# Full-array matmuls ahead of the scores in slots with few jobs: attention and a bilinear GLU on one core

## The chip, the core and the metric

The kernel runs on one core of a Trainium2 chip. The metric is the time of one execution on the device in microseconds, the median of several runs. Beside it stands one profiled execution with the records of every engine: TensorE (PE, with its weight loads as PEld), VectorE (DVE), ScalarE (ACT), GpSimd (POOL) and SyncE (SP), which issues the DMAs.

## The reference

One layer on x of 2048 rows and 640 columns, in bfloat16: attention with 32 heads of 20 columns behind a layer norm, then a bilinear GLU of inner width 1728 behind another.

```python
qkv = layernorm(x) @ wqkv                       # 3 x 32 heads x 20
p = softmax(q @ k.T * 20 ** -0.5)               # per head, 2048 x 2048
h = x + (p @ v) @ wo
g, u = layernorm(h) @ w_gate, layernorm(h) @ w_up
out = h + (g * u) @ w_down
```

## The kernel before, in words

Heads lie in eight groups of four, each head in a strip of 32 rows (20 used). For a group, a block of 512 queries and a tile of 128 keys, a score matmul takes one strip of kT as weights and one strip of the queries as moving data (L427); it uses a quarter of the array's rows, and the strips of different heads can run beside each other. Three such results of 512 columns (or six of 256 in the last passes) fill a **score tile** `sc` of 128 x 1536 in PSUM. There are two such tiles, so the scores of tile i wait until the exponential of tile i-2 has read its own. ScalarE turns each of the 656 score tiles into a tile E of exponentials (L433). A matmul per head and key tile then multiplies E by the values (L597, 32 output columns, a quarter of the array too) and sums in the bank `acc`, four in a batch.

The main loop takes one score tile per **slot**. In each slot it issues, in this order, the scores and the exponential (`emit_S`), goes on with an open job up to a budget of 640 nominal ns (`go_on`), issues a batch of value matmuls of an earlier tile (`emit_AV`), runs events that are due (the norms' DMAs) and pieces of VectorE work, and, where the job was at its end, begins another up to 440 nominal ns (`begin`) or one of the "x" pieces, which make some of the exponentials on VectorE from scores in the bank `mi` (L453 to L477). TensorE works in program order, so this is its order.

**Jobs** are all the other matmuls: projections of q and k (L270), of v (L284), transposes (L252), the output projection (L812), the GLU's two products (L878) and its last one (L911). They are generators that yield nominal costs: 216 for a matmul of 512 columns, 136 for one of 320, 300 for a job of five transposes, 680 for a job of v. Marks such as NEXT and END carry no cost. All jobs share one PSUM bank, `mi`, so the next one waits until VectorE has emptied it. `step` fetches the next cost from the current job. Jobs come in queues: projections first, then, when all norms of a block of queries are there, its tail (output projection, layer norm, GLU). Between a tail's end and the next block's norms there are few or none, as before the first transposes of a tail. The norms of the last groups of a pass run as urgent jobs with float32 matmuls (L539, L551).

`ident` is the 128 x 128 identity in bfloat16, `kT[0]` holds the keys of group 0 and is complete after the first chunks. `keep_busy(WARM)` (L640 to L643) issues 58 matmuls of the identity by itself into one place of a score tile before the loop, in the time in which the first input arrives. WARM, 58, also serves the change as the index of a tile. Behind the loop comes the last tail, with PSUM banks of its own.

## Time and profile before

| | |
|---|---|
| median of 3 runs | 977.72 us (975.7 to 977.83) |
| profiled execution, its span | 977.6 us |
| TensorE busy | 865.3 us (89%), 6981 matmuls recorded |
| ScalarE busy | 905.2 us (93%), of it exponentials 887.8 |
| VectorE busy | 576.8 us (59%) |
| scores L427 | 2352 matmuls, 1456 of them 32x512 |
| values L597 | 2432 matmuls |
| granted TensorE clock, mean over the span | 0.935 |

Busy times are unions of the records of an engine; the mean of one instruction can be longer than its distance from the next, as they overlap: one exponential lasts 1.66 us on record, and 656 of them fill 887.8 us. The row PEclk has the clock that the throttle granted to TensorE in 40 equal slices of 24.4 us, in tenths of full speed. In a list of waits, "A <- B" is idle time of A that ended when B was done.

### The profile page before, as it was taken

The page shows a single profiled execution, that of the slowest core. Times are in us where ns is not written, and L with a number is a line of the kernel's source. Part 1 is how long each engine was busy: PE and PEld are TensorE (multiplying, and loading weights), DVE is VectorE, ACT ScalarE, POOL GpSimd, SP SyncE. Part 2 cuts the span into 40 slices and gives each one's busy share as a digit, 9 for nine tenths or more (in the row PEclk, how much of TensorE's full clock was granted, in tenths as well). Part 3 has the DMA queues.
Part 4 walks back from the last instruction along what each step waited for, and adds up shares of the span by engine and source line. Part 5 has one row for each costly group of instructions (what it writes and reads, how often), then busy time and mean ns, then how long its engine had stood idle before and what let it go on. Part 6 is the DMA issues. An engine that isn't in the chain of part 4 may idle for free.

```text
span 977.6 us, 17623 instructions
## 1 busy us (share of the span) xinstructions
PE 865.3 (89%) x6981; PEld 325.1 (33%) x7041; DVE 576.8 (59%) x1186; ACT 905.2 (93%) x692; POOL 64.6 (7%) x163
## 2 busy tenths in 40 slices
PE   6779998889989899999898988898889999989987
PEld 4223332222223222233232222233332333435455
DVE  7564367877777777777677677777143331143232
ACT  6689999999999899999999999999899999999941
POOL 4110001200000000000000000000000000000000
PEclk9999999999999599999778899999597999989989
DMA  6000000010014022101420222000602000211210
GB/s 182 4 24 1 1 25 24 13 32 27 5 47 146 12 66 59 40 13 33 180 67 12 66 67 60 12 22 23 163 1 66 14 13 20 67 36 40 81 35 17
DMA packets 67816, 44.42 MB, mean 45 GB/s; under 512 B 18504, under 2 KB 63404, under 8 KB 67728
## 3 DMA queue, kind: packets, MB, share of 16 engines
q1 hardware_dynamic: 67728, 43.23, 15.5%
q8 instruction: 57, 0.93, 0.4%
q14 instruction: 31, 0.25, 0.1%
HBM read 35.91 MB, written 7.30 MB: 44 GB/s over the span
## 4 chain that ended last, share of the span: by engine, by line
ACT 44%; PE 32%; issue 13%; DVE 9%; POOL 1%; ACTq 0%; DVEq 0%; POOLq 0%
ACT E L433 44%; PE sc L427 8%; PE acc L597 6%; PE mi L878 3%; PE mi L270 3%; PE mi L812 2%; PE mi L284 2%; PE mi L911 2%; PE f L878 2%; DVE xv L463 1%; PE mi L453 1%; DVE st L176 1%; PE f L911 1%; PE mi L252 1%; DVE vx L239 1%
## 5 line engine op out<-in xcount | busy, mean ns | idle before, releaser
L433 ACT ACTIVATE E<-sc 128x1536 bf16<-128x1536 f32 x656 | 887.8, 1662 | 30.4 <-PE sc L427 29.7
L427 PE MATMUL sc<-qa,kT 32*128 32x512 bf16 x1456 | 205.9, 406 | 41.3 <-ACT E L433 35.0
L597 PE MATMUL acc<-E,vx 128*32 128x512 bf16 (+1 forms) x2352 | 215.6, 374 | 5.3 <-DVE vx L239 4.1
L427 PEld LDWEIGHTS <-kT 32*128 32x128 bf16 x2352 | 89.8, 92 | 260.8 <-issue 251.0
L597 PEld LDWEIGHTS <-vx 128*32 128x32 bf16 x2432 | 56.6, 94 | 159.7 <-issue 151.9
L270 PE MATMUL mi<-lnT,wp 128*128 128x512 bf16 x282 | 84.7, 382 | 9.7 <-DVE kT L277 2.3
L427 PE MATMUL sc<-qb,kT 32*128 32x256 bf16 (+1 forms) x896 | 72.0, 301 | 13.8 <-ACT E L433 13.0
L529 POOL TENSOR_TENSOR on<-asb,bc 128x512 bf16<-128x512 f32 (+1 forms) x30 | 34.5, 1150 | 714.7 <-DMA bc<-scr 507.1
L463 DVE TENSOR_SCALAR xv<-mi 128x512 int32<-128x512 f32 x80 | 55.0, 688 | 29.9 <-PE mi L453 26.3
L911 PE MATMUL mi<-wd,hh 128*128 128x320 bf16 x378 | 68.4, 303 | 3.6 <-DVE xv L463 3.5
L239 DVE CAST u<-mi 128x512 bf16<-128x512 f32 (+3 forms) x56 | 34.9, 624 | 56.2 <-PE mi L878 56.0
L886 DVE TENSOR_TENSOR hh<-mi,u 128x512 bf16<-128x512 f32 (+3 forms) x56 | 34.9, 624 | 55.0 <-PE mi L878 54.9
L878 PE MATMUL mi<-ln2T,wu 128*128 128x512 bf16 (+2 forms) x188 | 55.2, 385 | 4.6 <-DVE xv L463 3.0
L468 DVE SCALAR_TENSOR_TENSOR xe<-xt,xv 128x512 bf16<-128x512 f32 x80 | 56.6, 707 | 2.0
L477 DVE SCALAR_TENSOR_TENSOR xt<-xt,xm 128x512 f32<-128x512 f32 x80 | 56.3, 704 | 0.9
L476 DVE SCALAR_TENSOR_TENSOR xt<-xm 128x512 f32<-128x512 f32 x80 | 55.7, 697 | 0.0
L878 PE MATMUL mi<-ln2T,wg 128*128 128x512 bf16 (+2 forms) x187 | 52.3, 372 | 2.2 <-issue 0.8
L911 PEld LDWEIGHTS <-hh 128*128 128x128 bf16 x448 | 37.5, 97 | 40.1 <-issue 29.8
L915 DVE TENSOR_TENSOR xr<-mi,xr 128x320 bf16<-128x320 f32 x27 | 13.3, 492 | 51.3 <-PE mi L911 51.3
L812 PE MATMUL mi<-wo,on 128*128 128x320 bf16 x224 | 41.8, 311 | 0.7 <-DVE xv L463 0.4
L607 DVE COPY asb<-acc 128x512 f32<-128x512 f32 (+1 forms) x34 | 20.2, 594 | 34.5 <-PE acc L597 32.3
L277 DVE TENSOR_SCALAR kT<-mi,one_row 128x512 bf16<-128x512 f32 x31 | 23.2, 749 | 29.0 <-PE mi L270 29.0
(143 smaller groups left out, 637.0 us busy)
## 6 DMA issues: line engine op xcount, KB each, us to landing
bc<-scr SPq DMA_DIRECT2D x100, 64.0 KB
wu<-in_B_w_up_dram SPq DMA_DIRECT2D x20, 320.0 KB
wg<-in_B_w_gate_dram SPq DMA_DIRECT2D x20, 320.0 KB
qsp<-qa SPq DMA_DIRECT2D x8, 384.0 KB
xr<-in_A_x_dram SPq DMA_DIRECT2D x16, 160.0 KB
out_dram<-xr SPq DMA_DIRECT2D x14, 160.0 KB
wd<-in_B_w_down_dram SPq DMA_DIRECT2D x13, 160.0 KB
xs<-in_A_x_dram SPq DMA_DIRECT2D x3, 640.0 KB
```

The costliest lines, as they stand in the source:

```text
L239: nc.vector.tensor_copy(dst, src)
L270: nc.tensor.matmul(ps[:], lhsT=wslice(m, g, c), rhs=lnT[:, c, ch * QB:(ch + 1) * QB], start=(c == 0), stop=(c == KT - 1))
L427: nc.tensor.matmul(sc[:, o:o + w], lhsT=kT[g][SLOT * j:SLOT * (j + 1), kt * P:(kt + 1) * P], rhs=q_of(g, b, c0, w)[SLOT * j:SLOT * (j + 1) ...
L433: nc.scalar.activation(e[:, 0:n], sc[:, 0:n], ACT.Exp, bias=EXP_BIAS, scale=SM_SCALE)
L463: nc.vector.tensor_scalar(v[:], ps[:], X_SCALE, 0.0, ALU.mult, ALU.max)
L468: nc.vector.scalar_tensor_tensor(e[:], t[:], X_R, v[:].bitcast(F32), ALU.add, ALU.mult)
L476: (690, lambda: nc.vector.scalar_tensor_tensor(t[:], m[:], X_P, m[:], ALU.add, ALU.mult)),
L477: (690, lambda: nc.vector.scalar_tensor_tensor(t[:], t[:], X_Q, m[:], ALU.add, ALU.mult)),
L597: nc.tensor.matmul(acc["t"][SLOT * j:SLOT * (j + 1), 0:w], lhsT=vx[kt][:, VS * h:VS * h + SLOT], rhs=e, start=(acc["n"][j] == 0), stop=(ac ...
L812: nc.tensor.matmul(ps[:, 0:HALF], lhsT=on[g][:, t * P:(t + 1) * P], rhs=wo[g][:, cs], start=(g == 0), stop=(g == NG - 1))
L878: nc.tensor.matmul(ps[0:M, 0:n], lhsT=st["w", fp][k][:, c, f2 * P:f2 * P + M], rhs=st["ln2T"][:, c, c0:c0 + n], start=(c == 0), stop=(c == ...
L911: nc.tensor.matmul(ps[:, 0:HALF], lhsT=st["hh"][f][0:K, t * P:(t + 1) * P], rhs=late["Wd"][f][0:K, cs], start=(f == 0), stop=(f == 2 * FP ...
```

## The change

In `emit_S`, ahead of a tile's scores, one matmul of the full array (the identity as weights, the first 512 columns of `kT[0]` as moving data) is issued into the first bank of the same score tile if the tile's index is above 58, if the tile is at least 512 columns wide, and if the sum over the last three slots is below 600. A slot's entry in that sum is 213 if it got such a matmul, and the nominal costs of all steps of jobs in that slot. The scores then overwrite the bank (`start=True`). The rest of the kernel, the order of jobs too, is as before.

```diff
+HEAT = 600
...
+    heat = deque([0, 0, 0], maxlen=3)
+
     def step():
...
         cur["fresh"] = c in (END, NEXT)
+        if not cur["fresh"]:
+            heat[-1] += c
         return c
...
     def emit_S(i):
         sc = scp.tile([P, EW], F32, name="sc")
         us, n = tiles[i]
+        if i > WARM and sum(heat) < HEAT and n >= BANK:
+            nc.tensor.matmul(sc[:, 0:BANK], lhsT=ident[:], rhs=kT[0][:, 0:BANK], start=True, stop=True)
+            heat.append(BANK * 5 // 12)
+        else:
+            heat.append(0)
         for s, kt, j, _ in us:
```

## The prediction

> **What bounds the kernel now.** I read the busy shares first, then the costliest groups, then the waits, and last the stretches around the dips of the clock row. ScalarE is the bound: 656 exponentials over 128x1536 fill 887.8 of 977.6 us, and one follows the other at 1.33 us wherever the score tile is ready (median distance of the starts in the trace 1330 ns). The columns of a group are instructions, busy us, mean ns, and idle time before them with its main cause.

> ```profile
> ACT  6689999999999899999999999999899999999941
> ...
> PEclk9999999999999599999778899999597999989989
> ...
> L433 ACT ACTIVATE E<-sc 128x1536 bf16<-128x1536 f32 x656 | 887.8, 1662 | 30.4 <-PE sc L427 29.7
> ```

> The reader is to see that ScalarE lacks 30 us of work in the whole loop, nearly all of it waiting for TensorE's scores, and that the clock row falls to 5 to 8 tenths in a few slices. The list of waits gives the two sides (us in total, times, longest):

> ```profile
> PE sc L427 <- ACT E L433: 48.0, 123, 1.0
> ...
> ACT E L433 <- PE sc L427: 29.7, 38, 4.7
> ```

> TensorE waits more for ScalarE than the other way round; it has room on average and lacks it in places. The places are in the stretches. The lines below are TensorE alone, in steps of 3.4 us, because the trace's clock changes lie 3.41 us or multiples of it apart (3.4, 6.8, 10.2, 13.7, 20.5, 23.9 us). Columns: length, busy us with instructions, granted clock, DMA.

> ```profile
> 471.70:475.10 3.40, 3.10 (x27) 1.00 0.27 99
> 475.10:478.50 3.40, 1.51 (x17) 1.00 0.98 366
> 478.50:481.90 3.40, 2.67 (x15) 0.50 0.92 346
> ...
> 492.20:495.60 3.40, 3.40 (x19) 0.50 0.68 207
> 495.60:499.00 3.40, 3.40 (x19) 0.50 0.86 243
> 499.00:502.40 3.40, 3.30 (x27) 1.00 0.04 8
> ```

> One window with 17 matmuls, all of them strips, and the next has half the clock. It stays there until jobs are back. I counted this over the whole trace: each matmul's columns times the part of the array that it uses (a score strip of 32 rows or an L597 strip of 32 columns is a quarter), as a share of what full clock could stream in the window. Seventeen strips are 17 x 0.25 x 0.213 = 0.91 us, 0.27 of 3.41. In the exponentials' part, every full-clock window that half clock followed held at most 0.335 (at 563.9), every one that kept its clock at least 0.374 (at 659.4). So in this trace the clock is kept above about 0.355, an estimate from these two. Slots without jobs hold 0.22 to 0.30 over three tiles.

> What a slow stretch costs is seen on the matmuls (columns: start, us):

> ```profile
> 482.13 0.61 PE L427 MATMUL sc<-qa,kT 32*128 32x512 bf16 x3 [0.19 <-ACT E L433]
> ...
> 482.68 0.62 PE L597 MATMUL acc<-E,vx 128*32 128x512 bf16 x4
> ```

> Scores and values step by 0.55 us each at half clock; their two steps of 1.10 fit into 1.33. With jobs beside them they don't: at tiles with 300 to 650 ns of jobs the exponentials came 0.4 to 1.1 us late. After tile 58, ScalarE's distance above 1.33 us in and right behind half clock sums to 1.7 (290.8 to 297.6), 5.0 (321.5 to 342.0), 1.3 (478.5 to 499.0), 3.4 (529.7 to 543.4), 1.5 (567.3 to 570.7), 3.1 (683.3 to 707.2), 1.9 (734.5 to 744.8), 0.6 (867.6 to 874.5) and 0.7 (922.3 to 925.7): **19.2 us**, most of it at the end of a stretch, when jobs come back and the clock isn't back yet. That is all the change can win.

> **What the change adds.** Nothing is removed or moved. Going through TensorE's instructions in program order with the nominal costs that the jobs yield, the sum over three slots is below 600 at 44 of the tiles after 58: 3 around 288 to 291 us, 4 at 323 to 329, 12 at 477 to 496, 3 at 527 to 530, 14 at 680 to 707, 3 at 733 to 736, 1 at 853, 3 at 866 to 869 and 1 at 924; none before the stretch at 567. Thirty of them begin inside half clock. In a long gap three tiles of four get one.

> Cost of one at full clock: 512 columns take 0.22 us (three L878 matmuls in a row stand in 0.82 us, one alone in 0.38: 0.22 apart). The filler takes over the scores' wait for the exponential two tiles back; behind it on TensorE stand that tile's scores, then jobs, then L597, and only ScalarE and the job evictions wait for these. In a slot without jobs, TensorE waits for ScalarE anyway, and the scores are done 0.39 + 0.22 + 0.1 (a weight load) after the release, while the other exponential runs 1.33. So I take 0; without that cover it would be 44 x 0.32 = 14 us. It needs no wait towards the scores: the 58 warm-up matmuls of L642, which write one place again and again, stand in 4.68 us, 81 ns each. No DMA, no SP, POOL or DVE instruction is added.

> Cost of one at half clock: a third step of 0.55, so 1.65 against 1.33, 0.32 late at most; a free tile in four and the second score buffer take some of it up. Bounds 0 and 0.32; I take 0.2, nearer to the steps that the trace shows.

> Gain: one filler is 0.213/3.41 = 0.0625 of a window. With it the shares become 0.35 to 0.45 in most of the job-free slots. The first slots of a gap get none (the sum still holds the last jobs): at tiles 324 to 326 the windows hold 0.23 to 0.33 and the clock will still fall there, but one or two windows with three fillers lift it again instead of six. Stretch by stretch I take as saved 1.2 of 1.7, 3.5 of 5.0, 1.2 of 1.3, 2.4 of 3.4, 0 of 1.5 (no filler), 1.6 of 3.1 (2.2 of it is one float32 norm job, which halves at best), 1.3 of 1.9, 0.4 of 0.6 and 0.2 of 0.7: 11.8 us. About 11 windows of half clock remain, some 28 tiles, 17 of them with a filler: 17 x 0.2 = 3.4 us. Another 0.7 for fillers in slots whose own jobs fill them. Sum: 977.6 - 11.8 + 3.4 + 0.7 = 969.9. ScalarE's chain is unbroken to the last tile, so a saving there reaches the end; the last 45 us, behind the exponentials, are untouched. The profiled span is 0.1 below the median of 977.7, so **970 us**. The bounds of the parts (savings 7 to 17, costs 0 to 8) give 961 to 979.

> [...] The windows above lose their clock although TensorE never waits over 0.73 us in them. [...] The window from 522.9 to 526.3 keeps the clock with 0.41 where transposes are counted and 0.25 where they aren't. [...]

> **The rivals.**
> - *Slower: fillers that miss the threshold.* Two or three fillers bring a window from 0.25 to 0.37 or 0.44 against 0.355; if the chip counts a multiplication by the identity for less, or the threshold lies above 0.40 for such windows, the clock stays low and the 30 fillers inside half clock cost 0.32 each: 977.6 + 9.6 = 987. It decides from a weight of about half a filler. For it: half-clock windows up to 0.369 stayed low (335.2, 536.6). Against: the transposes, also identity matmuls, count in full.
> - *No change: the trailing edge stays.* The clock falls at the start of each gap, comes back, and falls again just before the jobs return, as the free-running windows happen to lie; savings of 4 against costs of 4, about 977. For it: margins of 0.02. Against: the long gaps have twelve and fourteen fillers up to the returning jobs.
> - *More: nearly all stretches keep full clock.* 19.2 less 1.5 and less the norm's 1.1, about 961. Against: the bare slots at the front.
> - *Fillers that miss what sets the clock.* If only a stretch with no matmul at all counts as idle, 44 fillers change nothing on the clock and cost 0 to 0.32 in the 30 places, some 3 us in all: 978 to 981. If transposes count as idle, the stretches that begin with them (321, 529, 734, 867) lose their 3.5 + 2.4 + 1.3 + 0.4 of savings: 977. Against both: the windows at 475.1 and 522.9.

> **How the numbers follow.** Forecast 970 (own range 966 to 974.5): 0.58. More, 961: 0.12. No change, 977: 0.14. Fillers that miss what sets the clock: 0.05 (0.03 at 978 to 981, 0.02 at 977). Slower, 987: 0.11. A difference below 0.3%, 2.9 us, can't be told from none here: faster 0.69, same 0.18, slower 0.13 (the upper edges of no change and of 978 to 981 add 0.02). The range of 8 in 10 reaches from the middle of "more" to "no change": 962 to 978.5.

> **What the profile after would show.** 44 more matmuls of 128x512 into the score tile; the clock row at 9 in the slices around 477 to 499 and 684 to 707 but for one or two windows; ScalarE's wait for the scores near 19 us instead of 29.7; the dip at 567 still there; half-clock windows after tile 58 down from 32 to about 11. Wrong would be: half clock in windows that hold 0.40 or more (the share is not what counts); an unchanged wait with a mended clock (the lateness had another cause); later exponentials at full clock right behind a filler (the cover isn't there).

## The result, and the profile after

The change made the kernel slower: 983.96 us against 978.46 (medians of 12 runs each), a ratio of 1.006, 95% interval 1.0037 to 1.0083. The forecast was 970 with a range of 962 to 978.5. The profiled execution has a span of 982.1 us; its own time is 984.0, so the span lies 1.9 below the time, where the prediction had put 0.1 between the span and the median.

The page after, clock row and exponentials; below them the list of waits:

```profile
PEclk9899999999999699999787999998597999999989
...
L443 ACT ACTIVATE E<-sc 128x1536 bf16<-128x1536 f32 x656 | 889.3, 1657 | 33.9 <-PE sc L437 33.0
```

```profile
ACT E L443 <- PE sc L437: 33.0, 44, 4.9
PE sc L437 <- ACT E L443: 32.3, 90, 0.9
```

The dips are where they were, and the wait that was to fall to 19 us rose from 29.7 to 33.0. TensorE waits less for ScalarE (32.3 after 48.0), so its room did go to the fillers. The filler's group (busy, mean ns, idle time before it) shows all 44:

```profile
L426 PE MATMUL sc<-kT,ident 128*128 128x512 bf16 x44 | 23.7, 538 | 8.5 <-ACT E L443 8.5
```

A mean of 538 ns, where such a matmul alone lasts 0.38 at full clock, says that most of them ran at half clock; 30 of the 44 start there. Between first and last exponential the two profiled executions differ by 5.1 us: 1.4 before tile 58, where no filler stands (half clock lay there for 10.2 us in place of 3.4, before 60 us), and 3.7 behind it. In the stretches of half clock, lateness changed by +2.2 (480 to 500), +4.0 (681 to 712), -1.9 (528 to 538) and at most 0.5 in each of the others. The gaps of the two stretches that grew hold 26 of the fillers, 23 of them at half clock: 6.2 us, or some 0.24 to 0.27 for each. Over all stretches of half clock it is 5.0 us for the 30.

The same stretch as in the prediction, TensorE alone (length, busy us with instructions, clock, DMA):

```profile
476.50:479.90 3.40, 1.81 (x15) 1.00 0.82 306
479.90:483.30 3.40, 3.40 (x19) 0.50 1.00 381
483.30:486.70 3.40, 2.76 (x16) 0.50 1.02 383
486.70:490.10 3.40, 3.40 (x23) 0.50 0.35 123
490.10:493.50 3.40, 3.40 (x17) 0.50 0.04 5
493.50:496.90 3.40, 3.40 (x17) 0.50 0.59 174
496.90:500.40 3.50, 3.50 (x16) 0.51 0.93 264
500.40:503.80 3.40, 3.40 (x28) 1.00 0.08 23
```

Six windows of half clock again, now with TensorE full in five of them, and the clock comes back only behind the sixth. A few slots of the next long gap show how that goes together (start, us):

```profile
682.49 0.62 PE L607 MATMUL acc<-E,vx 128*32 128x512 bf16 x4
683.04 0.61 PE L426 MATMUL sc<-kT,ident 128*128 128x512 bf16 x1
683.58 0.61 PE L437 MATMUL sc<-qa,kT 32*128 32x512 bf16 x3
...
684.55 0.61 PE L426 MATMUL sc<-kT,ident 128*128 128x512 bf16 x1
685.09 0.61 PE L437 MATMUL sc<-qa,kT 32*128 32x512 bf16 x3
685.63 0.62 PE L607 MATMUL acc<-E,vx 128*32 128x512 bf16 x4
686.18 0.61 PE L437 MATMUL sc<-qa,kT 32*128 32x512 bf16 x3
```

Filler, scores and values step by 0.55 us each, 1.65 for the three where the exponential takes 1.33. Counting 512 columns of the full array as 0.213 us at full clock, as the prediction does (two such matmuls in a row start 0.215 to 0.216 apart in both traces), they stream 0.213 for the filler, 0.16 for three strips of a quarter and 0.213 for four, 0.586 us of full-clock work; over 1.65 us that is a share of **0.355**. At these steps a slot of the three can't hold more at half clock, however many such slots follow each other; other matmuls and cut slots move a window a little. The highest shares counted in the long stretch from 681.3 on are 0.354 at 684.7, 0.358 at 688.1 and 0.363 at 698.3, and all stayed at half clock. The share does not explain every return, though. The window from 496.9 above holds only 0.28, with the same kinds of matmul, and the clock came back behind it; so it did behind 534.5 with 0.26, and in the profile before behind 703.8 with 0.25 and 922.3 with 0.32 (these two hold float32 matmuls of L551, counted by their columns like the others). Why is not shown.

### The profile page after: what moved, and what is told of

It reads as the page before. It is cut to its first block, busy times and chain, and to the rows that moved or that the text cites. A ratio compares the mean times of both kernels' runs of the same rounds, so it can differ in the third digit from the quotient of the medians.

```text
span 982.1 us, 17711 instructions
## 1 busy us (share of the span) xinstructions
PE 882.9 (90%) x7025; PEld 326.4 (33%) x7085; DVE 575.3 (59%) x1186; ACT 906.9 (92%) x692; POOL 64.0 (7%) x163
## 4 chain that ended last, share of the span: by engine, by line
ACT 43%; PE 35%; issue 12%; DVE 8%; POOL 1%; DMA 0%; ACTq 0%; DVEq 0%; POOLq 0%
ACT E L443 42%; PE sc L437 9%; PE acc L607 7%; PE mi L888 3%; PE mi L271 3%; PE mi L285 2%; PE mi L822 2%; PE sc L426 2%; PE f L888 2%; PE mi L921 1%; PE mi L463 1%; DVE xv L473 1%; DVE st L177 1%; PE f L921 1%; DVE kT L278 1%
## 5 line engine op out<-in xcount | busy, mean ns | idle before, releaser
L443 ACT ACTIVATE E<-sc 128x1536 bf16<-128x1536 f32 x656 | 889.3, 1657 | 33.9 <-PE sc L437 33.0
L437 PE MATMUL sc<-qa,kT 32*128 32x512 bf16 x1456 | 205.5, 406 | 29.7 <-ACT E L443 23.6
L437 PEld LDWEIGHTS <-kT 32*128 32x128 bf16 x2352 | 87.1, 92 | 253.7 <-issue 244.5
L484 DVE TENSOR_SCALAR xm<-xv 128x512 int32<-128x512 int32 x80 | 39.1, 488 | 2.7
```

The lines of the kernel that those rows point to most:

```text
L437: nc.tensor.matmul(sc[:, o:o + w], lhsT=kT[g][SLOT * j:SLOT * (j + 1), kt * P:(kt + 1) * P], rhs=q_of(g, b, c0, w)[SLOT * j:SLOT * (j + 1) ...
L443: nc.scalar.activation(e[:, 0:n], sc[:, 0:n], ACT.Exp, bias=EXP_BIAS, scale=SM_SCALE)
L484: (430, lambda: nc.vector.tensor_scalar(m[:].bitcast(I32), v[:], 0x007FFFFF, 0x3F800000, ALU.bitwise_and, ALU.bitwise_or)),
```

## The experiments

Theory A: a filler counts in full for the clock, but one in three of four slots is too little and begins too late; once the clock is at half, filler, scores and values fill TensorE below the share at which the clock comes back, and each filler then only costs. Theory B, the rival: a multiplication by the identity hardly counts, or something else than the streamed area sets the clock. All kernels start from the changed one. Half-clock windows are those of 3.41 us between tile 58 and the last exponential in the profiled execution, and lateness is ScalarE's distance above 1.33 us per exponential in the same part.

**One filler in each slot of a gap, one slot earlier.**

```diff
-HEAT = 600
+HEAT = 900
```

> The bound of the sum over three slots goes from 600 to 900: by the bookkeeping 67 fillers in place of 44, one in every slot of a gap, the first of them one slot earlier. Theory A (a filler counts in full for the clock, but three of four slots give a window share of 0.36 only, under the 0.37 to 0.38 at which the clock was kept, and once the clock is at half, score, filler and value steps of 0.55 us each fill TensorE at a share of 0.35, so that the clock can't come back): shares at full clock of 0.40, half-clock windows from 32 to 10 to 18, time 965 to 978. Theory B (a multiplication by the identity hardly counts): 32 half-clock windows as before, and 23 more fillers at 0.25 us make it some 5 us slower than the changed kernel, 986 to 990.

Measured: 984.55 us against 979.72, ratio 1.0051 (1.0031 to 1.0072); 23 half-clock windows, lateness 33.5 us. The windows fell less than theory A said, and the time not at all, so it lies far outside theory A's 965 to 978: 67 fillers (mean 489 ns on record, so many still at half clock) cost what the 44 had cost. Theory B's 32 windows it is not. The first windows of two gaps still held 0.295 (286.1) and 0.323 (320.3) and lost the clock; others lost it at 0.359 (477.3) and 0.375 (682.1), so the bare front is not all of it.

**Two fillers at the same places.**

```diff
             nc.tensor.matmul(sc[:, 0:BANK], lhsT=ident[:], rhs=kT[0][:, 0:BANK], start=True, stop=True)
+            nc.tensor.matmul(sc[:, BANK:2 * BANK], lhsT=ident[:], rhs=kT[0][:, 0:BANK], start=True, stop=True)
```

> Two fillers in place of one at the same 44 places, into the first and the second bank of the score tile. Theory A: at half clock a slot is 0.55 + 0.98 + 0.55 = 2.08 us with a share of 0.385, enough to bring the clock back after one or two windows; half-clock windows from 32 to 12 to 20, time 972 to 982. Theory B: 32 half-clock windows or more, each filler in them costs 0.7 us in place of 0.25, time 993 to 1003.

Measured: 979.96 us, ratio 1.001 (0.9978 to 1.0041); 15 half-clock windows, lateness 30.0. Twice the fillers, and no slower than with none, where B asked for 993 us or more. That it is faster than with one filler is likely, but the two intervals touch (up to 1.0041 here, from 1.0037 there). TensorE in the stretch of before:

```profile
478.00:481.40 3.40, 1.67 (x12) 1.00 1.00 383
481.40:484.80 3.40, 3.40 (x16) 0.50 1.01 377
484.80:488.20 3.40, 2.76 (x15) 0.50 1.01 386
488.20:491.70 3.50, 3.50 (x18) 0.51 0.21 68
491.70:495.10 3.40, 2.46 (x20) 1.00 0.07 17
```

The clock is back after three windows, not six, with no job in them (one x piece stands at 483.10). Two slots of it:

```profile
486.82 0.58 PE L426 MATMUL sc<-kT,ident 128*128 128x512 bf16 x1 [0.64 <-ACT E L444]
487.20 0.63 PE L427 MATMUL sc<-kT,ident 128*128 128x512 bf16 x1
487.76 0.61 PE L438 MATMUL sc<-qa,kT 32*128 32x512 bf16 x3
488.30 0.62 PE L608 MATMUL acc<-E,vx 128*32 128x512 bf16 x4
488.86 0.61 PE L426 MATMUL sc<-kT,ident 128*128 128x512 bf16 x1
```

From filler to filler 2.04 us, in which 0.80 us of work is streamed: 0.39, against 0.355 with one. The stretch from 324.4 to 344.9 kept its six windows; there, transposes of 300 hold the sum above 600 and few fillers are issued.

**Data as weights in place of the identity.**

```diff
-            nc.tensor.matmul(sc[:, 0:BANK], lhsT=ident[:], rhs=kT[0][:, 0:BANK], start=True, stop=True)
+            nc.tensor.matmul(sc[:, 0:BANK], lhsT=kT[0][:, 0:P], rhs=kT[0][:, 0:BANK], start=True, stop=True)
```

> The same 44 fillers with the keys of group 0 as weights in place of the identity, so that the array multiplies data everywhere. Theory A: as the changed kernel, 32 half-clock windows, 981 to 986. Theory B (the identity hardly counts): the clock now stays up, half-clock windows 10 to 16, time 968 to 975.

Measured: 985.7 us, ratio 1.0056 (1.0029 to 1.0083); 31 half-clock windows, lateness 35.7. As the changed kernel: what is multiplied makes no difference here. B's first form falls.

**A quarter of the columns.**

```diff
-            nc.tensor.matmul(sc[:, 0:BANK], lhsT=ident[:], rhs=kT[0][:, 0:BANK], start=True, stop=True)
+            nc.tensor.matmul(sc[:, 0:P], lhsT=ident[:], rhs=kT[0][:, 0:P], start=True, stop=True)
```

> The same 44 places, but 128 columns in place of 512. Both theories: 31 to 33 half-clock windows. If the loss is the time that a filler takes on TensorE at half clock (0.43 us of stream and 0.12 of step), the step is now 0.23 us and fits into the 0.23 us that a slot has left (1.10 against 1.33): time 978 to 980. If the loss comes with each filler whatever its length (a wait, a weight load, a lost overlap of strips), 982 to 985.

Measured: 978.96 us, ratio 0.9995 (0.9974 to 1.0017); 32 half-clock windows, lateness 29.0. Lines of two slots at half clock:

```profile
484.15 0.61 PE L437 MATMUL sc<-qa,kT 32*128 32x512 bf16 x3
484.69 0.62 PE L607 MATMUL acc<-E,vx 128*32 128x512 bf16 x4
485.29 0.26 PE L426 MATMUL sc<-kT,ident 128*128 128x128 bf16 x1
485.49 0.61 PE L437 MATMUL sc<-qa,kT 32*128 32x512 bf16 x3
```

The step of a filler is 0.20 us and the slot 1.34, just what ScalarE takes. The loss of the change is thus the filler's length at half clock, not a wait or a weight load that comes with each.

**Two fillers, and the bound 900**: both edits above together.

```diff
-HEAT = 600
+HEAT = 900
...
             nc.tensor.matmul(sc[:, 0:BANK], lhsT=ident[:], rhs=kT[0][:, 0:BANK], start=True, stop=True)
+            nc.tensor.matmul(sc[:, BANK:2 * BANK], lhsT=ident[:], rhs=kT[0][:, 0:BANK], start=True, stop=True)
```

> Two fillers per slot and the bound 900: 67 places, one slot earlier in each gap, 134 fillers. Theory A (area counts; one filler was too little, and the first slots of a gap got none): shares above 0.40 from the second or third slot of a gap on, half-clock windows behind tile 58 from 32 to 4 to 12, lateness of the exponentials behind tile 58 from 30 to 17 to 24 us, time 966 to 976. If fillers at full clock cost as much as the clock brings: half-clock windows as few, but 977 to 983.

Measured: 971.12 us against 976.84, ratio 0.993 (0.9908 to 0.9951), faster than both kernels; 4 half-clock windows, lateness 21.8. Clock row and wait:

```profile
PEclk9998999999999999999999999999999999999999
```

```profile
ACT E L444 <- PE sc L438: 24.6, 25, 4.5
```

The dips at 14, 20, 21, 29 and 31 of the forty slices are gone. Slots of the old half-clock stretch (where the second filler's record is missing, its weight load is in the trace):

```profile
483.92 0.39 PE L426 MATMUL sc<-kT,ident 128*128 128x512 bf16 x1
484.14 0.38 PE L427 MATMUL sc<-kT,ident 128*128 128x512 bf16 x1
484.45 0.39 PE L438 MATMUL sc<-qa,kT 32*128 32x512 bf16 x3
484.77 0.40 PE L608 MATMUL acc<-E,vx 128*32 128x512 bf16 x4
```

Here filler, scores and values take 0.22 + 0.31 + 0.32 + 0.34 = 1.19 us with two fillers, inside 1.33. Lateness outside half clock is 12.1 us against 10.5 before, so 134 fillers, nearly all at full clock, cost about 1.6 us there, if nothing else became shorter.

**Two fillers by the jobs of two slots alone.**

```diff
-HEAT = 600
+HEAT = 301
...
-    heat = deque([0, 0, 0], maxlen=3)
+    heat = deque([0, 0], maxlen=2)
...
-            heat.append(BANK * 5 // 12)
-        else:
-            heat.append(0)
+            nc.tensor.matmul(sc[:, BANK:2 * BANK], lhsT=ident[:], rhs=kT[0][:, 0:BANK], start=True, stop=True)
+        heat.append(0)
```

> Two fillers in each slot behind two slots whose jobs add to at most 300, fillers not counted: some 72 places, among them the slots between the transposes in front of a tail, where the count of 600 left gaps. Theory A: as the two fillers with the bound 900, and the stretch around 324 to 345 now keeps its clock for the most part: half-clock windows 3 to 10, time 966 to 976.

Measured: 969.85 us, ratio 0.9925 (0.9903 to 0.9947); 6 half-clock windows, lateness 24.6. Not to be told from the one above. The stretch at 324 to 345 kept its clock in both.

**The same time on TensorE, less area.** Each filler is two matmuls of one 32-row strip.

```diff
-            nc.tensor.matmul(sc[:, 0:BANK], lhsT=ident[:], rhs=kT[0][:, 0:BANK], start=True, stop=True)
+            r0 = SLOT * us[0][2]
+            for _ in range(2):
+                nc.tensor.matmul(sc[:, 0:BANK], lhsT=kT[0][r0:r0 + SLOT, 0:P], rhs=kT[0][r0:r0 + SLOT, 0:BANK], start=True, stop=True)
```

> At the 44 places of the change, two matmuls of one strip of 32 rows and 512 columns, one behind the other, in place of one full-array matmul: twice the time on TensorE, half the area. If area times columns is what the clock is kept by (theory A): 31 to 36 half-clock windows, each pair costs some 0.7 us at half clock, time 988 to 1002. If the time counts in which TensorE streams at all, whatever the area: as with two full-array fillers, 12 to 20 half-clock windows, 975 to 984.

Measured: 999.45 us, ratio 1.022 (1.0192 to 1.0248); 40 half-clock windows, more than the 31 to 36 of theory A, lateness 49.1. Its clock row, and a slot at half clock:

```profile
PEclk9889999989998599999768999998597999979989
```

```profile
490.92 0.58 PE L428 MATMUL sc<-kT 32*128 32x512 bf16 x1 [0.64 <-ACT E L445]
490.93 0.61 PE L439 MATMUL sc<-qa,kT 32*128 32x512 bf16 x2
491.30 0.63 PE L428 MATMUL sc<-kT 32*128 32x512 bf16 x1
...
492.83 0.60 PE L428 MATMUL sc<-kT 32*128 32x512 bf16 x1
```

The filler's strips run beside strips of the scores where their rows differ (the first two start at 490.92 and 490.93), and the slot is 1.91 us long, against 1.65 with one full-array filler. TensorE is busy for longer than in the changed kernel (901 us, 883), and its clock over the runs is lower (0.916 to 0.927, 0.922 to 0.942). More time on TensorE alone did not keep the clock, so B's second form falls as it was put here. That streamed area keeps it is what the counted windows bear out, within the limits named below.

| kernel | fillers per slot, bound | half-clock windows | lateness, us | ratio to before | granted clock, all runs |
|---|---|---|---|---|---|
| before | none | 32 | 30.2 | 1 | 0.926 to 0.938 |
| the change | 1, 600 | 31 | 33.9 | 1.006 | 0.922 to 0.942 |
| earlier | 1, 900 | 23 | 33.5 | 1.0051 | 0.944 to 0.956 |
| double | 2, 600 | 15 | 30.0 | 1.001 | 0.951 to 0.972 |
| data as weights | 1, 600 | 31 | 35.7 | 1.0056 | 0.930 to 0.941 |
| quarter of the columns | 1 short, 600 | 32 | 29.0 | 0.9995 | 0.926 to 0.935 |
| both | 2, 900 | 4 | 21.8 | 0.993 | 0.978 to 0.987 |
| by the jobs of two slots | 2 | 6 | 24.6 | 0.9925 | 0.979 to 0.987 |
| strips | 2 strips, 600 | 40 | 49.1 | 1.022 | 0.916 to 0.927 |

Windows and lateness come from one profiled execution of each kernel; the mean granted clock of every run, in the last column, bears the windows out.

## Why the prediction was wrong, point by point

- *The bound.* Right. Half-clock windows make the exponentials late, and taking nearly all of them away (32 to 4) took 8.4 us of lateness away in the profiled executions.
- *The 44 fillers and their places.* Right: 44 records, in the stretches named, none at 567.
- *A filler counts in full, 0.0625 of a window.* Nothing here speaks against it at full clock: identity and data act alike (31 half-clock windows each), and pairs of strips, which have half the area, do not help (40).
- *"With it the shares become 0.35 to 0.45 ... one or two windows with three fillers lift it again instead of six."* **This step failed**, and with it the largest term of the sum, 11.8 us of savings: 31 windows of half clock stayed where about 11 were forecast, and in the stretches of half clock lateness rose by 5.0 us. The shares were worked out by laying the fillers onto windows whose slots last 1.33 us. At half clock the slot grows to 1.65 us and holds about 0.355, so the fillers that were to lift the clock lengthened the slot instead. Two fillers, with 0.39 in a slot, brought the clock back after three windows in one long stretch, which fits; the returns at 0.25 to 0.32 named above do not, so what leaving half clock takes is only in part explained.
- *The threshold.* 0.355, taken from one trace as the middle between 0.335 and 0.374, was too sharp. In the changed kernel's trace windows of 0.369 and 0.373 (288.7, 322.9) lost the clock, each with fillers in it, and one of 0.348 (869.0) kept it; over all nine traces full-clock windows between about 0.32 and 0.38 went either way. Three fillers in four slots add 0.12 to the 0.22 to 0.30 of slots without jobs: 0.34 to 0.42, an estimate, and much of it lies inside this band. The half-clock windows up to 0.369 that stayed low in the profile before said so already; they stand in the prediction under the rival alone.
- *The front of the gaps gets no filler.* Right, and it weighed more than was taken: one filler per slot did not undo the entry (23 half-clock windows), and only the kernels with two fillers and an earlier or a different count kept the clock in nearly all gaps (4 and 6).
- *Cost 0 at full clock.* Nearly right: some 1.6 us for 134.
- *Cost 0.2 at half clock.* Right in size (0.24 to 0.27 in the two stretches that grew), but 30 fillers, not 17, ran at half clock.
- *The slower rival* had the way the loss came about, 30 fillers paying at half clock, and one of its conditions, a threshold that one filler does not clear; the identity as a reason was wrong, and its price of 30 x 0.32 = 9.6 was too high. Measured were 3.7 us behind tile 58 in the profiled executions and 0.6% in the medians.
- *The longest wait, 0.73 us.* The longest wait of TensorE in the prediction's windows was 0.95 us (it ends at 478.10), not 0.73; that they lost the clock with short waits alone stands with it. The kernel with strips is one more case: TensorE was busy for longer, its longest wait in the two longest stretches of half clock was 0.9 us, and 40 windows were at half clock.

Still open: the 1.4 us before tile 58, where the kernels do the same. The eight other profiled executions have 16.0 to 17.9 us of lateness there, the one of before 14.7; the half-clock windows lie differently, but why was not tried. The band of the threshold is open too: the share counts starts and columns as recorded, some records are missing and were put back from the weight loads, and no run here shows what sets the clock. The third open point is the way back from half clock, as said above.

## What to carry to other kernels

In this kernel, filler work that was to hold the clock had to be enough by a margin and be there before the clock fell: half the dose cost 0.6%, the double dose one slot earlier gained 0.7%. Work out what the engine can reach at half clock, too: there, one late filler per slot only lengthened the slots (1.65 us against 1.33). Count activity by streamed area (strips, with half the area in twice the time, had 40 half-clock windows in place of 31), and take a threshold from all windows, at full and at half clock, before anything is built on a margin of 0.02.
